# Sparse attention and a token mix on one core: stores and loads of x by 32 rows, two tiles of normalised sums, the mix's first steps in the fixed order, and a weight decode with an addition by GpSimd

## The chip, the cores and the metric

The kernel runs on one core of a Trainium2 chip. A core has five engines that work side by side, each through its own instructions in order: TensorE (PE, with its weight loads shown apart as PEld), VectorE (DVE), ScalarE (ACT), GpSimd (POOL) and SyncE (SP), which here only issues transfers. Sixteen DMA engines move data between the device's memory and SBUF. The metric is the device time of one execution in microseconds. Three timed runs of the kernel before gave 680.64, 686.46 and 686.54 us (median 686.46).

## What is computed

Block-sparse attention over 4 batches, 8 heads, 768 positions and head size 64, followed by a token mix over x, the attention's output with its heads side by side (512 channels). Positions fall into 24 blocks of 32. A query block sees its neighbours, the first and the last block, and three sampled blocks; the first and the last query block see everything.

```python
scores = scale * np.matmul(q, k.transpose(0, 1, 3, 2))
mask = np.abs(blk_i - blk_j) <= window                     # window = 1
mask = mask | (blk_i == 0) | (blk_j == 0) | (blk_i == n_blocks - 1) | (blk_j == n_blocks - 1)
# ... and the three sampled key blocks of each query block
scores = np.where(mask, scores, -1000000000.0)
attn = np.exp(scores - np.max(scores, axis=-1, keepdims=True))
attn = attn / (np.sum(attn, axis=-1, keepdims=True) + 1e-09)
x = np.matmul(attn, v)                                     # heads side by side: (4, 768, 512)

theta = x @ w_theta
zr, zi = x * np.cos(theta), x * np.sin(theta)
y = np.einsum('ts,bsd->btd', w_tok_r, zr) + np.einsum('ts,bsd->btd', w_tok_i, zi)
u = x + y
out = u + np.maximum(u @ w_ch, 0.0)
```

All inputs are float32, but the four weight matrices of the mix reach the core as 64-bit words (two 32-bit words for each value) and are decoded there, each into a high and a low part, whose products (three for each matrix product) give nearly full precision.

## The kernel before

**Attention.** The 4 batches are two pairs `bp`. For each pair there are four *wide* units (the first and last query block, which see all 24 key blocks: one unit for each batch `b` and half of the heads `pp`) and 22 units `i` of one inner query block, all 16 heads of the two batches at once. The list `units` holds these 52 in order, and the loop over `n` runs them in software-pipelined steps under `manual_schedule`: within it the order of the code is the order on each engine. In step `n`:

- `gather_k(n + 2)` copies the key blocks of a unit from the resident `kb` into `kg` (POOL), and `gather_v(n + 2)` fetches the value rows by an indirect DMA that POOL issues (L265);
- `scores(n + 1)` multiplies (S, L282), VectorE reduces to the row bound `m` (L285), and `weights(n + 1)` takes exponentials on ScalarE (P, L294);
- `turn(n)` transposes the weights on PE (T, L300), and ScalarE copies them to `pT` (L302);
- in odd units `values` multiplies the weights of the last two units with their values (X, L333), a *round* of two units; `finish` adds 1e-9 to the row sums, takes the reciprocal and multiplies into the tile `xo` (L319), which exists once (`bufs=1`, L317), and SP stores it to `xs` in the device's memory in two DMAs of 64 rows (L350), each over two query blocks. The store of the wide units (L405) is cut the same way.

SP also issues, in the order of the steps, the loads of q, of the adjoining values (`va`), of the resident keys (`kb`, L222; the second pair's four loads reuse the first pair's space) and of the weights' words.

**The decode of the weights.** `Piece` turns 512 columns (256 for `w_ch`) of 64-bit words into high and low parts. The Decoder spreads three phases a piece over the steps: `ahead` issues `start` (ScalarE, L63) and `high` (ScalarE's cast, L80) before the step's scores, `go` issues `bits`, `rest` and `low` (VectorE, L67 to L84) after its transposes. Seven VectorE operations a piece: three in `bits`, two in `rest` (L75, L77), two in `low` (L83, L84). 22 pieces are decoded in attention and 8 (`w_ch`) in the mix. A piece's words are loaded when the piece two before has ended its third phase.

**The token mix** is a generator, `token_mix`. Its first part allocates what fits while attention's left pools still exist, loads x for two steps (`load_raw` as rows by head for the transposes, L560; `load` as tokens, L547), and does `turn(0)`, `turn(1)`, `theta(0)`, `theta(1)`; after a yield it opens the remaining pools in attention's memory and runs 48 steps (batch, half of the channels, block of 128 tokens): `theta` (L586 to L588), the angles' sine and cosine, `turned` (x times these, split in two parts), and `mix` (L624 to L626) into four accumulators, at each half's end `add_x`; `out` multiplies with `w_ch` (L647 to L649) and stores. This part's order is made by a planner with a cost model. The first part is called (`next(follow)`, L514) after the fixed order has ended, so the planner also places it among attention's last instructions.

`load` reads, for one step, four DMAs by head group `p`: 128 rows of 128 floats; `xs` is laid out as [pair, block, 2, 32 rows, batch, 2, 128].

Of the kernel before, what the change touches and what calls it, by code (L numbers as in the profile page):

```python
# [25 lines left out]
Q_BUFS = 3  # L26
RAW_AHEAD = 6
# [18 lines left out]
class Piece:  # L46
# [14 lines left out]
    def start(self):  # L61
        self.a = self.pool.tile([P, self.f], F32, tag="da", name=f"da_{self.name}", bufs=2)
        self.nc.scalar.activation(self.a, self.raw[:, :, 1].bitcast(F32), AF.Abs, scale=2.0**-16)  # L63

    def bits(self):
        nc, a, ai = self.nc, self.a, self.a.bitcast(I32)
        nc.vector.tensor_scalar(a, a, WORD_LO, WORD_HI, op0=ALU.max, op1=ALU.min)  # L67
        nc.vector.tensor_scalar(ai, ai, 4, 1, op0=ALU.logical_shift_left, op1=ALU.logical_shift_right)
        nc.vector.scalar_tensor_tensor(ai, self.raw[:, :, 1], SIGN_BIT, ai, op0=ALU.bitwise_and, op1=ALU.bitwise_or)

    def rest(self):

        nc = self.nc
        s = self.pool.tile([P, self.f], I32, tag="ds", name=f"ds_{self.name}")
        nc.vector.tensor_scalar(s, self.a.bitcast(I32), EXP_BITS, None, op0=ALU.bitwise_and)  # L75
        low = self.raw[:, :, 0]
        nc.vector.scalar_tensor_tensor(low.bitcast(F32), low.bitcast(U32), 2.0**-52, s.bitcast(F32), op0=ALU.mult, op1=ALU.mult)  # L77
# [4 lines left out]
    def low(self):  # L82
        self.nc.vector.tensor_tensor(self.a, self.a, self.hi.bitcast(F32), op=ALU.subtract)  # L83
# [33 lines left out]
class Tables:  # L117


    def __init__(self, nc, cp, sampled):  # L120
        self.raw = cp.tile([P, NB * 6], I32, name="sb_raw")
        nc.sync.dma_start(self.raw, sampled.rearrange("i k -> (i k)").partition_broadcast(P))

    def make(self, nc, cp):
        raw = self.raw
        words = raw.rearrange("p (i k w) -> p i k w", k=3, w=2)
        given = cp.tile([P, 3, NB], F32, name="sb_given")
        nc.vector.tensor_copy(given, words[:, :, :, 0].rearrange("p i k -> p k i"))
        r = cp.tile([P, 3, NB], F32, name="sb_r")
# [655 lines left out]
```

## Time and profile before

| | before |
|---|---|
| timed runs | 680.64, 686.46, 686.54 us, median 686.46 |
| profiled execution | 681.48 us, its span 679.7 us |
| instructions | 16671 |
| PE busy | 576.1 us (85%) |
| VectorE busy | 448.6 us (66%) |
| ScalarE busy | 334.9 us (49%) |
| POOL busy | 140.6 us (21%) |
| DMA | 95.57 MB, mean 141 GB/s |

The span is what the hardware profiler saw of one execution; 1.8 us lie around it. Busy shares are means over two stages that differ: POOL and most of the DMA traffic belong to attention, and the mix is TensorE's. In the profile a line such as "51.21 0.70 DVE xo L319" gives start, duration, engine, tile and line; what stands in brackets after a timeline entry is the idle time before it and who ended it. "SPq" is the issue of a transfer by SP.

### The profile page before, as it was taken

What the parts mean: (1) busy time and instruction counts of PE and PEld (TensorE: products, weight loads), DVE (VectorE), ACT (ScalarE), POOL (GpSimd) and SP (SyncE); (2) the same over time, 40 slices, a digit from 0 to 9 for tenths busy, and PEclk for the clock granted to TensorE, in tenths of its full rate; (3) what the DMA queues carried; (4) which work ended last, traced back from release to release, by engine and by line L of the source; (5) the groups of instructions that cost most, each with busy time, mean ns of one, the idle gap of its engine ahead of it and who ended that gap; (6) DMA issues with size and microseconds to landing.
All of it is one profiled execution on the core that took longest, in us unless ns stands there. A gap on an engine that the chain in (4) does not pass through costs nothing.

```text
span 679.7 us, 16671 instructions
## 1 busy us (share of the span) xinstructions
PE 576.1 (85%) x6592; PEld 501.7 (74%) x6592; DVE 448.6 (66%) x1063; ACT 334.9 (49%) x708; POOL 140.6 (21%) x262
## 2 busy tenths in 40 slices
PE   4788767585878777774879999999999999999996
PEld 2466445462655545543769999999999999999996
DVE  3797775463777657655389979666586765846654
ACT  3466546362656455544266575345553455533520
POOL 1457546322247454620000000000000000000000
PEclk9989789786989879995769999999999999999999
DMA  8778668665579656742344323421133211121102
GB/s 300 257 224 237 212 208 261 219 213 191 175 231 274 194 180 201 250 140 78 92 123 120 107 56 83 123 78 59 48 95 108 68 58 47 60 69 62 31 0 94
DMA packets 71110, 95.57 MB, mean 141 GB/s; under 512 B 5240, under 2 KB 52984, under 8 KB 71032
## 3 DMA queue, kind: packets, MB, share of 16 engines
q1 hardware_dynamic: 64696, 71.08, 33.3%
q0 software_dynamic: 6336, 23.43, 10.6%
q8 instruction: 52, 0.85, 0.5%
q14 instruction: 26, 0.21, 0.1%
HBM read 81.90 MB, written 12.58 MB: 139 GB/s over the span
## 4 chain that ended last, share of the span: by engine, by line
PE 48%; DMA 34%; DVE 10%; SPq 3%; ACT 3%; issue 2%; DVEq 0%; ACTq 0%
DMA xs<-xo 26%; PE y L624 9%; PE y L625 9%; PE y L626 9%; PE h L588 3%; PE h L586 3%; PE h L587 3%; PE o L647 3%; PE o L648 3%; PE o L649 3%; PE SW L367 3%; DMA kb<-in_kT_dram 2%; DVE xo L319 2%; SPq L350 2%; DMA va<-in_vr_dram 1%
## 5 line engine op out<-in xcount | busy, mean ns | idle before, releaser
L243 POOL COPY kg<-kb 128x256 f32 (+2 forms) x202 | 94.9, 510 | 62.2 <-PE S L282 25.7
L294 ACT ACTIVATE P<-S,m 128x256 f32<-128x256 f32 x176 | 69.1, 477 | 77.4 <-DVE m L285 69.9
L300 PE MATMUL T<-ident,P 128*128 128x128 f32 x352 | 56.3, 312 | 19.9 <-ACT pT L302 19.4
L586 PE MATMUL h<-w_theta_hi,xTh 128*128 128x256 f32 x192 | 56.7, 295 | 14.9 <-ACT P L294 11.7
L624 PE MATMUL y<-w_tok_r_hi,zh 128*128 128x384 f32 x192 | 66.1, 344 | 3.7 <-DVE xo L319 3.3
L300 PEld LDWEIGHTS T<-ident,P 128*128 128x128 f32 x352 | 45.1, 160 | 31.9 <-ACT pT L302 28.9
L333 PE MATMUL X<-vb,pT 128*32 128x65 f32 x1408 | 45.0, 244 | 24.9 <-DVE xo L319 24.8
L625 PE MATMUL y<-w_tok_r_lo,zh 128*128 128x384 f32 x192 | 65.6, 342 | 0.0
L626 PE MATMUL y<-w_tok_r_hi,zl 128*128 128x384 f32 x192 | 64.8, 337 | 0.0
L625 PE MATMUL y<-w_tok_i_lo,zh 128*128 128x384 f32 x192 | 64.7, 337 | 0.0
L624 PE MATMUL y<-w_tok_i_hi,zh 128*128 128x384 f32 x192 | 64.7, 337 | 0.0
L265 POOL DMA_INDIRECT vb<-in_vr_dram,rows x44 | 43.8, 995 | 93.0 <-PE X L333 87.4
L626 PE MATMUL y<-w_tok_i_hi,zl 128*128 128x384 f32 x192 | 62.2, 334 | 0.0
L302 ACT COPY pT<-T 128x1024 f32<-128x1024 f32 x44 | 44.9, 1020 | 33.5 <-PE T L300 33.2
L285 DVE TENSOR_REDUCE m<-S 128x2 f32<-128x512 f32 x88 | 56.2, 680 | 5.9 <-PE S L282 5.9
L333 PEld LDWEIGHTS X<-vb,pT 128*32 128x32 f32 x1408 | 28.5, 119 | 42.0 <-DVE xo L319 32.0
L319 DVE TENSOR_TENSOR xo<-X,sm 128x512 f32<-128x512 f32 x22 | 15.2, 692 | 64.9 <-DMA xs<-xo 62.7
L588 PE MATMUL h<-w_theta_hi,xTl 128*128 128x256 f32 x192 | 56.3, 293 | 1.4 <-DVE xTl L578 1.4
L587 PE MATMUL h<-w_theta_lo,xTh 128*128 128x256 f32 x192 | 56.0, 292 | 0.0
L282 PE MATMUL S<-kg,q 64*32 64x256 f32 x1408 | 53.0, 410 | 3.3 <-DVE q L217 2.0
L586 PEld LDWEIGHTS h<-w_theta_hi,xTh 128*128 128x128 f32 x192 | 38.3, 199 | 16.1 <-ACT P L294 11.9
L333 PE MATMUL X<-va,pT 128*64 128x65 f32 x704 | 44.6, 255 | 0.7 <-DMA va<-in_vr_dram 0.6
(127 smaller groups left out, 1303.6 us busy)
## 6 DMA issues: line engine op xcount, KB each, us to landing
xa<-xs SPq DMA_DIRECT2D x192, 64.0 KB
vw<-in_vr_dram SPq DMA_DIRECT2D x8, 780.0 KB
kb<-in_kT_dram SPq DMA_DIRECT2D x8, 768.0 KB
xr<-xs SPq DMA_DIRECT2D x96, 64.0 KB
out_dram<-of SPq DMA_DIRECT2D x32, 192.0 KB
va<-in_vr_dram SPq DMA_DIRECT2D x22, 260.0 KB
q<-in_qT_dram SPq DMA_DIRECT2D x22, 256.0 KB
xs<-xo SPq DMA_DIRECT2D x44, 128.0 KB
```

Of the source, the lines that this page charges most:

```text
L243: nc.gpsimd.tensor_copy(dst, blocks.rearrange("r g s f -> r s g f"))
L282: nc.tensor.matmul(sc[32 * p : 32 * p + 32, e, b, :], q[rows, b, p, :], keys[rows, :, :, 4 * b + p, :], start=True, stop=True)
L285: nc.vector.tensor_reduce(m[:, e], sc[:, e], axis=AX.X, op=ALU.min)
L294: nc.scalar.activation(pt[:, e, b, :], sc[:, e, b, :], AF.Exp, bias=m[:, e, b : b + 1], scale=-1.0)
L300: nc.tensor.transpose(t[:, k, :], pt, ident)
L333: nc.tensor.matmul(x[r0 : r0 + 32 * n, b, 2 * (p // 2) + e, :], pT_pair[:, 4 * c + 2 * e + b, p, u0 : u0 + n, :], v[:, v0 : v0 + 65], star ...
L586: nc.tensor.matmul(ps, hi[:, c, :], wh[:, c, :], start=c == 0, stop=False)
L587: nc.tensor.matmul(ps, hi[:, c, :], wl[:, c, :], start=False, stop=False)
L588: nc.tensor.matmul(ps, lo[:, c, :], wh[:, c, :], start=False, stop=c == 3)
L624: nc.tensor.matmul(acc, zh[:, dd], wh[:, j, tt], start=j == 0 and m == 0, stop=False)
L625: nc.tensor.matmul(acc, zh[:, dd], wl[:, j, tt], start=False, stop=False)
L626: nc.tensor.matmul(acc, zl[:, dd], wh[:, j, tt], start=False, stop=j == 5 and m == 1)
```

## The change

- `xo` has two buffers. `Tables`, small work at the start, puts its scratch tiles into one of them.
- The stores of `xo` are cut into four DMAs of 32 rows, one for each query block and half of the partitions, where there were two of 64. Heads are regrouped: the half of the partitions is now `p // 2` (before, `p % 2`), and a row of `xs` holds the heads accordingly; keys and values are laid out by the host to match (`place`, `kT`, `va`).
- The mix's `load` is four DMAs of 32 rows with two runs of 256 floats a row, where each had 128 rows of 128 floats.
- The first part of `token_mix` is split by a further yield and moved into the fixed order: pools and the sixteen loads at step `n == len(units) - 2`; `turn`, the load of the sine table, and `theta` of steps 0 and 1 in the last unit's step, before its `finish`.
- The decode: ScalarE makes a second tile from the lower words (`Copy` with a scale, to an integer), `bits` puts the sign into that tile, and `rest` is one integer addition on GpSimd in place of two VectorE operations; `low` is one VectorE operation in place of two. VectorE has four operations a piece. The words of a piece are loaded when the piece two before has done its `bits`.

```diff
+XO_BUFS = 2
@@ Piece
     def start(self):
-        self.nc.scalar.activation(self.a, self.raw[:, :, 1].bitcast(F32), AF.Abs, scale=2.0**-16)
+        self.nc.scalar.activation(self.a, self.raw[:, :, 1].bitcast(F32), AF.Abs, scale=2.0**-48)
+        self.r = self.pool.tile([P, self.f], I32, tag="ds", name=f"ds_{self.name}")
+        self.nc.scalar.activation(self.r, self.raw[:, :, 0].bitcast(U32), AF.Copy, scale=2.0**-29)
     def bits(self):
         nc.vector.tensor_scalar(a, a, WORD_LO, WORD_HI, op0=ALU.max, op1=ALU.min)
-        nc.vector.tensor_scalar(ai, ai, 4, 1, op0=ALU.logical_shift_left, op1=ALU.logical_shift_right)
-        nc.vector.scalar_tensor_tensor(ai, self.raw[:, :, 1], SIGN_BIT, ai, op0=ALU.bitwise_and, op1=ALU.bitwise_or)
+        nc.vector.tensor_scalar(ai, ai, 3, None, op0=ALU.logical_shift_left)
+        nc.vector.scalar_tensor_tensor(r, self.raw[:, :, 1], SIGN_BIT, r, op0=ALU.bitwise_and, op1=ALU.bitwise_or)
     def rest(self):
-        nc.vector.tensor_scalar(s, self.a.bitcast(I32), EXP_BITS, None, op0=ALU.bitwise_and)
-        low = self.raw[:, :, 0]
-        nc.vector.scalar_tensor_tensor(low.bitcast(F32), low.bitcast(U32), 2.0**-52, s.bitcast(F32), op0=ALU.mult, op1=ALU.mult)
+        ai = self.a.bitcast(I32)
+        self.nc.gpsimd.tensor_tensor(ai, ai, self.r, op=ALU.add)
     def low(self):
-        self.nc.vector.tensor_tensor(self.a, self.a, self.hi.bitcast(F32), op=ALU.subtract)
-        self.nc.vector.tensor_tensor(self.lo, self.a, self.raw[:, :, 0].bitcast(F32), op=ALU.add)
+        self.nc.vector.tensor_tensor(self.lo, self.a, self.hi.bitcast(F32), op=ALU.subtract)
@@ Decoder.go
-            if k % 3 == 2 and k // 3 + 2 < len(self.pieces):
+            if k % 3 == 0 and k // 3 + 2 < len(self.pieces):
                 self.pieces[k // 3 + 2].load(self.pool, self.queue)
@@ Tables
-        self.raw = cp.tile([P, NB * 6], I32, name="sb_raw")
+        self.scratch = wp.tile([P, 8, 64], F32, tag="xo", name="sb_scratch", bufs=XO_BUFS).rearrange("p g d -> p (g d)")
+        self.raw = self.part(0, NB * 6).bitcast(I32)
...
@@ attention
-    with ExitStack() as ctx, ExitStack() as early:
+    with ExitStack() as ctx, ExitStack() as scored, ExitStack() as early:
-        ps_s = early.enter_context(tc.tile_pool(name="ps_s", bufs=2, space=PSUM, side="right"))
+        ps_s = scored.enter_context(tc.tile_pool(name="ps_s", bufs=2, space=PSUM, side="right"))
+        def place(b, p):
+            return 4 * b + 2 * (p % 2) + p // 2
-            xo = wp.tile([P, 8, 64], F32, tag="xo", name=f"xo{name}", bufs=1)[:, 0:n]
+            xo = wp.tile([P, 8, 64], F32, tag="xo", name=f"xo{name}", bufs=XO_BUFS)[:, 0:n]
@@ finish
             for c in range(2):
-                nc.sync.dma_start(xs[bp, i : i + 2, c].rearrange("u q b p f -> u q (b p f)"), xo[64 * c : 64 * c + 64])
+                for u in range(2):
+                    r0 = 64 * c + 32 * u
+                    nc.sync.dma_start(xs[bp, i + u, c].rearrange("q b p f -> q (b p f)"), xo[r0 : r0 + 32])
@@ finish_wide
-                    nc.sync.dma_start(xs[bp, 0 : NB : NB - 1, c, :, b].rearrange("z q p f -> z q (p f)"), xo[64 * c : 64 * c + 64])
+                    for z in range(2):
+                        r0 = 64 * c + 32 * z
+                        nc.sync.dma_start(xs[bp, (NB - 1) * z, c, :, b].rearrange("q p f -> q (p f)"), xo[r0 : r0 + 32])
@@ the loop over the steps
             for n in range(len(units) + 1):
+                if n == len(units) - 2:
+                    early.close()
+                    next(follow)
...
                     decoder.go(phases)
+                    if n == len(units) - 1:
+                        scored.close()
+                        next(follow)
                     if last:
                         finish(*last)
...
-        early.close()
-        next(follow)
@@ token_mix
-        ps_h = ctx.enter_context(tc.tile_pool(name="ps_h", bufs=3, space=PSUM, side="right"))
-        ps_o = ctx.enter_context(tc.tile_pool(name="ps_o", bufs=1, space=PSUM, side="right"))
-        tc.keep_in_program_order(nc.scalar.activation(early, half_pi, AF.Sin))
@@ load
-            for p in range(4):
-                src = xs[b // 2, 4 * j : 4 * j + 4, p % 2, :, b % 2, p // 2]
-                nc.sync.dma_start(xa[k][:, p].rearrange("s c u -> s (c u)"), src)
+            for i in range(4):
+                src = xs[b // 2, 4 * j + i, :, :, b % 2].rearrange("c q p f -> q c (p f)")
+                dst = xa[k][32 * i : 32 * i + 32].rearrange("s (c p) x u -> s c (p x u)", c=2)
+                nc.sync.dma_start(dst, src)
@@ the first part
         for k in range(2):
             load_raw(k, xp)
             load(k)
+        yield
+        ps_h = ctx.enter_context(tc.tile_pool(name="ps_h", bufs=3, space=PSUM, side="right"))
+        ps_o = ctx.enter_context(tc.tile_pool(name="ps_o", bufs=1, space=PSUM, side="right"))
         turn(0)
         turn(1)
+        nc.scalar.activation(early, half_pi, AF.Sin)
         theta(0)
         theta(1)
         yield
```

More of the change, by code (lines that the diff above doesn't have):

```diff
@@ L26 @@
 Q_BUFS = 3
+XO_BUFS = 2
 RAW_AHEAD = 6
-WORD_LO = float(np.array([768 << 20], np.uint32).view(np.float32)[0])
-WORD_HI = float(np.array([(1022 << 20) | 0xFFFFF], np.uint32).view(np.float32)[0])
+WORD_LO = float(np.array([512 << 20], np.uint32).view(np.float32)[0])
+WORD_HI = float(np.array([(766 << 20) | 0xFFFFF], np.uint32).view(np.float32)[0])
 SIGN_BIT = -(1 << 31)
-EXP_BITS = -(1 << 23)
 C1 = 6.28125
@@ L117, with __init__, part @@
 class Tables:
-    def __init__(self, nc, cp, sampled):
-        self.raw = cp.tile([P, NB * 6], I32, name="sb_raw")
+    def __init__(self, nc, wp, sampled):
+        self.scratch = wp.tile([P, 8, 64], F32, tag="xo", name="sb_scratch", bufs=XO_BUFS).rearrange("p g d -> p (g d)")
+        self.raw = self.part(0, NB * 6).bitcast(I32)
         nc.sync.dma_start(self.raw, sampled.rearrange("i k -> (i k)").partition_broadcast(P))
+    def part(self, c0, n):
+        return self.scratch[:, c0 : c0 + n]
     def make(self, nc, cp):
@@ L126, in make @@
         words = raw.rearrange("p (i k w) -> p i k w", k=3, w=2)
-        given = cp.tile([P, 3, NB], F32, name="sb_given")
+        given = self.part(144, 72).rearrange("p (k i) -> p k i", k=3)
         nc.vector.tensor_copy(given, words[:, :, :, 0].rearrange("p i k -> p k i"))
-        r = cp.tile([P, 3, NB], F32, name="sb_r")
+        r = self.part(216, 72).rearrange("p (k i) -> p k i", k=3)
         nc.vector.tensor_scalar(r, given, 0.0, float(NB - 1), op0=ALU.max, op1=ALU.min)
@@ L132, in make @@
         nc.vector.tensor_copy(self.block.rearrange("p (i k) -> p k i", k=3), r[0:1])
-        iota_i = cp.tile([P, NB], I32, name="iota_i")
+        iota_i = self.part(288, NB).bitcast(I32)
         nc.gpsimd.iota(iota_i, pattern=[[1, NB]], base=0, channel_multiplier=0)
-        qi = cp.tile([P, NB], F32, name="qi")
+        qi = self.part(312, NB)
         nc.gpsimd.tensor_copy(qi, iota_i)
@@ L141, in make @@
             nc.gpsimd.memset(rows[96:128, :, i], int(ZEROS))
-        first_i = cp.tile([96, NP], I32, name="first_i")
+        first_i = self.part(336, NP)[0:96].bitcast(I32)
         for k in range(3):
             nc.gpsimd.iota(first_i[32 * k : 32 * k + 32], pattern=[[768, NP]], base=0, channel_multiplier=1)
-        first = cp.tile([96, NP], F32, name="first_row")
+        first = self.part(338, NP)[0:96]
         nc.gpsimd.tensor_copy(first, first_i)
@@ L281, in scores @@
                         rows = slice(64 * e, 64 * e + 64)
-                        nc.tensor.matmul(sc[32 * p : 32 * p + 32, e, b, :], q[rows, b, p, :], keys[rows, :, :, 4 * b + p, :], start=True, stop=True)
+                        nc.tensor.matmul(sc[32 * p : 32 * p + 32, e, b, :], q[rows, b, p, :], keys[rows, :, :, place(b, p), :], start=True, stop=True)
             m = wp.tile([P, 2, 2], F32, tag="m", name=f"m{bp}_{i}", bufs=3)
@@ L329, in values, with weigh @@
             va = vas[((i - 1) // 2) % VA_BUFS]
-            def weigh(b, e, p, c, u0, n, v, start, stop):
-                r0 = 64 * (p % 2) + 32 * u0
-                v0 = 65 * (8 * b + 4 * (p // 2) + 2 * e + p % 2)
+            def weigh(b, e, p, k, u0, n, v, start, stop):
+                c, pp = p // 2, p % 2
+                r0 = 64 * c + 32 * u0
+                v0 = 65 * (8 * b + 4 * pp + 2 * e + c)
                 nc.tensor.matmul(
-                    x[r0 : r0 + 32 * n, b, 2 * (p // 2) + e, :], pT_pair[:, 4 * c + 2 * e + b, p, u0 : u0 + n, :], v[:, v0 : v0 + 65],
+                    x[r0 : r0 + 32 * n, b, 2 * pp + e, :], pT_pair[:, 4 * k + 2 * e + b, p, u0 : u0 + n, :], v[:, v0 : v0 + 65],
                     start=start, stop=stop,
@@ L339, in values @@
                 for pp in range(2):
-                    heads = [(b, e, 2 * pp + c) for b in range(2) for c in range(2)]
+                    heads = [(b, e, 2 * c + pp) for b in range(2) for c in range(2)]
                     for head in heads:
@@ L365, in scores_wide @@
                     for e in range(2):
-                        rows, p = slice(64 * e, 64 * e + 64), 2 * pp + c
+                        rows, p = slice(64 * e, 64 * e + 64), 2 * c + pp
                         nc.tensor.matmul(
-                            scs[e][64 * c : 64 * c + 64, 32 * c0 : 32 * (c0 + n)], qe[rows, b, p, :], kb[rows, 4 * b + p, c0 : c0 + n, :],
+                            scs[e][64 * c : 64 * c + 64, 32 * c0 : 32 * (c0 + n)], qe[rows, b, p, :], kb[rows, place(b, p), c0 : c0 + n, :],
                             start=True, stop=True,
```

12 lines of the change are left out of this document (5 added, 7 removed).

## The prediction

> **What bounds the kernel now.** I read the page's chain of waits first, since busy shares are averages over two stages that differ: attention (0 to about 325 us), then the token mix.
>
> ```profile
> PE 48%; DMA 34%; DVE 10%; SPq 3%; ACT 3%; issue 2%; DVEq 0%; ACTq 0%
> DMA xs<-xo 26%; PE y L624 9%; PE y L625 9%; PE y L626 9%; PE h L588 3%; PE h L586 3%; PE h L587 3%; PE o L647 3%; PE o L648 3%; PE o L649 3%; PE SW L367 3%; DMA kb<-in_kT_dram 2%; DVE xo L319 2%; SPq L350 2%; DMA va<-in_vr_dram 1%
> ```
>
> A quarter of the span runs through the stores of `xo`. The table of stretches separates the stages (columns: length, then busy time and count of PE, PEld, DVE, ACT, POOL, granted clock, DMA share, GB/s):
>
> ```profile
> 50.00:299.00 249.00, 187.38 (x3730) 129.71 (x3728) 160.37 (x296) 132.39 (x248) 122.77 (x217) 0.87 0.67 215
> 400.00:500.00 100.00, 100.00 (x630) 100.00 (x629) 70.59 (x190) 50.49 (x119) 0.00 (x0) 1.00 0.26 76
> ```
>
> The mix is TensorE without a gap at full clock: nothing done to its loads or decode can shorten its steady part. In attention no engine is full; PE is busy 75% at clock 0.87. The chain in order of time shows why, and the list of waits who pays:
>
> ```profile
> 51.21 0.70 DVE xo L319
> 51.93 0.51 SPq L350
> 52.50 9.97 DMA xs<-xo
> 62.59 0.70 DVE xo L319
> ```
>
> ```profile
> POOL vb L265 <- PE X L333: 87.4, 19, 10.9
> ACT P L294 <- DVE m L285: 69.9, 34, 8.1
> DVE xo L319 <- DMA xs<-xo: 62.7, 17, 8.8
> ```
>
> With one `xo` tile, L319 waits until the previous store has landed. Behind it in VectorE's order stands the reduction `m`, behind that ScalarE's exponentials, and PE's X waits for the sums tile that L319 frees. A round (two units: 2 S, 2 T, one X) is thus 0.70 + 0.51 + about 10 us.
>
> The timeline gives the length of rounds with and without that wait, from the T that follows each X:
>
> ```profile
> 49.98 1.09 PE L300 MATMUL T<-ident,P 128*128 128x128 f32 x8
> 57.46 1.09 PE L300 MATMUL T<-ident,P 128*128 128x128 f32 x8
> 149.40 1.09 PE L300 MATMUL T<-ident,P 128*128 128x128 f32 x8
> 206.71 1.09 PE L300 MATMUL T<-ident,P 128*128 128x128 f32 x8
> 214.20 1.09 PE L300 MATMUL T<-ident,P 128*128 128x128 f32 x8
> 302.84 1.09 PE L300 MATMUL T<-ident,P 128*128 128x128 f32 x8
> ```
>
> 49.98 to 149.40 are nine rounds of 11.05 us, 206.71 to 302.84 nine of 10.68: mean 10.86. The first round of each half, in which L319 meets no large store in flight, took 7.48 and 7.49 us. That is the round which this PE order reaches when nothing blocks it.
>
> **The stores.** Two edits meet here: two tiles, and 32 rows by store. Two tiles alone only let a store take two rounds. Whether the transfer itself gets shorter is read where little else moves (issues with KB each, then the chain at the end of attention and of the kernel):
>
> ```profile
> xs<-xo SPq DMA_DIRECT2D x44, 128.0 KB
> out_dram<-of SPq DMA_DIRECT2D x32, 192.0 KB
> ```
>
> ```profile
> 318.13 7.96 DMA xs<-xo
> 328.74 7.69 DMA xs<-xo
> 669.07 1.85 DMA out_dram<-of
> ```
>
> A pair's 256 KB took 7.7 to 8.0 us there, against 1.85 us for 192 KB over 128 partitions: near 33 against 104 KB per us. The narrow path is the store's own, not the memory. Old stores begin with a dimension of 2 (`u`, or `z`), new ones with 32 rows. I take the new pair's store at the other row's rate, 256/104 = 2.5 us (bounds 1.85 and 8.0), well inside two rounds. The Trainium skill (DMA: Bandwidth & Descriptors, section on why a DMA increments its semaphore by 16, "How many engines") says that the engine count is the largest number up to 16 dividing the slowest dimension of both sides. By that rule the old stores used 2 engines and the new use 16; the 33 against 104 agrees, though no row counts engines.
>
> **The decode.** Rows by line, for 512-column pieces:
>
> ```profile
> L75 DVE TENSOR_SCALAR ds_tok_r<-da_tok_r 128x512 int32<-128x512 int32 x9 | 4.0, 448 | 0.1
> L77 DVE SCALAR_TENSOR_TENSOR raw_tok_r<-raw_tok_r,ds_tok_r 128x512 f32<-128x512 uint32 x9 | 6.4, 711 | 0.3
> L83 DVE TENSOR_TENSOR da_tok_r<-da_tok_r,w_tok_r_hi 128x512 f32<-128x512 f32 x9 | 7.0, 776 | 0.0
> L63 ACT ACTIVATE da_tok_r<-raw_tok_r 128x512 f32<-128x512 f32 x9 | 6.3, 702 | 0.0
> L243 POOL COPY kg<-kb 128x512 f32<-128x512 f32 x26 | 17.1, 668 | 36.5 <-DMA kb<-in_kT_dram 20.9 <-DMA q<-in_qT_dram 15.5
> ```
>
> VectorE loses three of seven operations: 0.45 + 0.71 + 0.78 = 1.94 us a piece. ScalarE gains one like L63, 0.70 us. POOL gains an integer addition, which the trace doesn't show. Two groups of the same five copies, and a round of POOL without a blocked store:
>
> ```profile
> 230.81 1.98 POOL L243 COPY kg<-kb 128x512 f32<-128x512 f32 x5
> ```
>
> ```profile
> 206.69 0.96 POOL L265 DMA_INDIRECT vb<-in_vr_dram,rows  x1 [2.73 <-PE X L333]
> 207.65 2.04 POOL L243 COPY kg<-kb 128x256 f32<-128x256 f32 x4
> 209.84 0.97 POOL L265 DMA_INDIRECT vb<-in_vr_dram,rows  x1 [0.16 <-issue]
> 210.82 3.13 POOL L243 COPY kg<-kb 128x512 f32<-128x512 f32 x5
> ```
>
> Bounds of the addition: below, 0.67 us (POOL's copy of this size, one input); above, 2 x 0.67 x 3.13/1.98 = 2.1 us, two inputs in the crowded form. I take two inputs, 1.34, nearer to the uncrowded row. By the Trainium skill (GPSIMD Engine Reference, side-by-side accounting: 4497 ns at 2048 elements, VectorE half that) an estimate is 1.1 us, and that page advises VectorE for such work; the sum would move by under 4 us.
>
> 22 pieces make 66 phases over a weight of 56 (44 units, six wide ones counting 2): 66/56 x 2/3 = 0.79 pieces a round. So per round VectorE -1.5 us, ScalarE +0.55, POOL +1.06. POOL's unblocked round above, 206.69 to 213.95, is 7.26 us, with the additions 8.3. New waits: the addition waits for VectorE's `bits`, with the key copies and gathers queued behind it on POOL; ScalarE's cast `high` waits for the addition, with exponentials behind. Mostly these phases lie a unit apart, which covers both. The raw load now waits on `bits` instead of `low`, earlier. SP issues two more stores a round, 2 x 0.51 us, with `va` and `q` loads behind; POOL's and PE's order leave them a round to land.
>
> **Round after:** between PE's 7.5 and POOL's 8.3 I take 8.2. The others fit, scaling the stretch 50:299 by 10.86/8.2 = 1.32: DMA 0.67 to 0.89, VectorE 0.64 to 0.85 less 0.19, ScalarE 0.53 to 0.70 plus 0.07. Gain: 18 x (10.86 - 8.2) = **48 us** (7.5: 60; 9.3: 28).
>
> **The second wide stage** (the chain, then PE in the timeline):
>
> ```profile
> 146.00 0.51 SPq L350
> 147.78 11.53 DMA kb<-in_kT_dram
> ```
>
> ```profile
> 159.44 2.96 PE L367 MATMUL SW<-kb,qe 64*64 64x512 f32 x16 [8.95 <-DMA kb<-in_kT_dram]
> ```
>
> SP issues these keys only after the store at 146.00, which itself waited for L319, and they land beside it. Without the wait they go out a few us earlier relative to PE's work and don't share the store's path: of 8.95 I take **8** (2 to 9). Cheaper decode ahead of the row sums in the two wide stages: at most 1.94 each, **3** (0 to 4).
>
> **The mix's first steps.** In the timeline (PE and VectorE):
>
> ```profile
> 311.18 0.89 DVE L576 STREAM_TRANSPOSE r<-xr 128x128 f32<-128x128 f32 x4 [8.26 <-DMA xr<-xs]
> 315.58 0.58 PE L586 MATMUL h<-w_theta_hi,xTh 128*128 128x256 f32 x1 [11.65 <-ACT P L294]
> 328.28 0.66 PE L624 MATMUL y<-w_tok_r_hi,zh 128*128 128x384 f32 x1 [3.33 <-DVE xo L319]
> ```
>
> The planner put the transposes ahead of the last reduction; they waited for loads not yet landed, and PE stood 11.65 us. The change issues the sixteen loads a round earlier, when key space is free, and turns and multiplies after the last T. From the last T row to the first mix matmul were 25.4 us; without that wait 13.8. Sixteen issues at about 0.5 us now stand on SP ahead of the store of the pair before the last; the second tile covers that. Theta stands ahead of the last X: if the loads are late, X waits too and the gain is gone. I take **11.5** (5 to 13).
>
> ```profile
> 340.00:350.00 10.00, 6.50 (x28) 5.29 (x27) 9.61 (x35) 5.67 (x13) 0.00 (x0) 0.69 0.37 92
> ```
>
> Here 28 matmuls ran where the steady mix runs 63, some 5.5 us lost, because the next loads waited for the store at 328.74 (7.69 us) whose memory they reuse, and VectorE was full. A shorter store and decode give **4** (0 to 7). Wider elements in `xa` loads: nothing, PE covers them.
>
> **Sum:** 48 + 8 + 3 + 11.5 + 4 = 74.5, from the profiled execution's 681.5 (span 679.7): 607. Its runs were 680.6 to 686.5, median 686.5, so the profile sits at the low end; allowing 2 of those 5 us, **609**.
>
> **Rivals.**
> - *The additions land on the path.* POOL is the fullest engine by this sum, and while its copies ran the slow forms appeared (3.13 us above). If each addition also holds up VectorE for its length, the round is 7.26 + 0.79 x 2 x 1.34 = 9.4: 18 x 1.46 + 26.5 = 53 gained, **629**. The Trainium skill (SBUF — State Buffer, port-pair lock) makes VectorE's two-input operations and POOL exclude each other. Against: VectorE has room and drops two such operations. 0.2.
> - *Stores stay narrow.* Then each round still pushes 8 us of store through a path that loads share, the round stays near 10, kb and early mix gain nothing: 18 x 0.86 + 14.5 = 30, **651**. The two rates above speak against. 0.08.
> - *Slower:* a slow integer addition on POOL, in front of gathers and copies. The gains are gone when 18 x (7.26 + 0.79t - 10.86) = 26.5, at t = 6.4 us; at 10 us it ends near **732**. No POOL row here is that long; but none is an integer addition of two tensors. 0.04.
> - *No change:* another wait of 10 us replaces the store's. The 7.48 us rounds speak against. 0.04.
>
> **Numbers.** Forecast 0.64 (594 to 620). The range 594 to 640 adds the first rival. Three runs spread by 0.9%, so 1% is what can be told: faster 0.92, within 1% 0.04, slower 0.04.
>
> **What would show it.** In the profile after: no wait of L319 on `xs<-xo`; T rows 8.2 us apart; a quiet store under 3 us; the addition near 1.3 us; SW's wait for `kb` under 2 us; first mix matmul about 14 us after the last pair's T; the stretch 400:500's density unchanged. Wrong if rounds stay over 9.5, if POOL shows idle time charged to VectorE's `bits` ahead of its gathers, or theta still waits for `xr`.

## The result, and the profile after

The changed kernel takes 620.12 us (median of 4 runs, 617.19 to 624.08), against 686.5 for the kernel before in its 4 runs (680.64 to 690.85): a ratio of 0.906 with a 95% interval of 0.8975 to 0.915. The forecast was 609, its range 594 to 640. The profiled execution took 618.81 us, its span 616.9; before these were 681.48 and 679.7, so 62.8 us of span went.

The chain of waits after, by engine and by line; the stores, which carried 26% before, are no longer among its first lines:

```profile
PE 67%; DVE 11%; DMA 8%; ACT 5%; issue 4%; POOL 2%; POOLq 1%; SPq 1%; DVEq 0%; ACTq 0%
PE y L636 10%; PE y L637 10%; PE y L638 10%; PE X L340 7%; PE T L306 4%; PE S L288 4%; PE h L600 3%; PE h L598 3%; PE h L599 3%; PE o L659 3%; PE o L661 3%; PE o L660 3%; PE SW L376 3%; ACT pT L308 2%; DVE q L219 2%
```

The table of stretches after, with the columns of the one before:

```profile
50.00:299.00 249.00, 210.94 (x4085) 152.91 (x4064) 170.14 (x336) 169.12 (x332) 145.39 (x239) 0.93 0.77 240
400.00:500.00 100.00, 100.00 (x634) 100.00 (x634) 66.56 (x177) 50.18 (x120) 0.00 (x0) 1.00 0.24 71
```

The steady mix runs 634 matmuls in 100 us where it ran 630: unchanged, as forecast. The first row spans the end of attention too, which comes earlier now, so it is not a row of like work. Rows of like work are the two runs of nine rounds and the first 30 us from the first mix matmul, before and then after:

```profile
49.98:149.40 99.42, 76.58 (x1588) 53.75 (x1585) 63.20 (x118) 52.50 (x102) 52.19 (x94) 0.85 0.69 220
206.71:302.84 96.13, 74.00 (x1589) 51.44 (x1585) 63.31 (x118) 52.07 (x102) 53.90 (x94) 0.91 0.65 208
328.28:358.28 30.00, 25.43 (x115) 24.02 (x116) 18.87 (x64) 13.20 (x32) 0.00 (x0) 0.68 0.39 110
```

```profile
48.59:130.51 81.92, 68.98 (x1589) 47.47 (x1585) 56.85 (x103) 57.69 (x115) 61.38 (x102) 0.98 0.92 286
182.40:260.48 78.08, 68.71 (x1588) 47.47 (x1585) 57.68 (x99) 56.69 (x112) 61.44 (x102) 0.98 0.82 255
277.53:307.53 30.00, 30.00 (x186) 30.00 (x187) 25.48 (x82) 21.12 (x55) 4.50 (x6) 0.94 0.59 168
289.25:299.25 10.00, 10.00 (x71) 10.00 (x70) 9.72 (x33) 8.38 (x24) 2.21 (x3) 1.00 0.64 180
```

In the rounds PE stands still for 22 us where it stood for 45, and the same matmuls take 137.7 us of PE where they took 150.6, at a granted clock of 0.98 against 0.85 and 0.91. So about a third of what the rounds gained came with the higher clock. The last row begins 11.7 us after the first mix matmul, as the prediction's 340:350 did before: 71 matmuls run there in place of 28.

The timeline of PE after, at the ends of the stages that the prediction sums:

```profile
48.59 1.09 PE L306 MATMUL T<-ident,P 128*128 128x128 f32 x8
130.51 1.09 PE L306 MATMUL T<-ident,P 128*128 128x128 f32 x8
133.62 1.94 PE L376 MATMUL SW<-kb,qe 64*64 64x512 f32 x5 [2.02 <-DMA kb<-in_kT_dram]
182.40 1.09 PE L306 MATMUL T<-ident,P 128*128 128x128 f32 x8
260.48 1.09 PE L306 MATMUL T<-ident,P 128*128 128x128 f32 x8
262.73 1.09 PE L306 MATMUL T<-ident,P 128*128 128x128 f32 x8 [1.16 <-ACT pT L308]
265.50 0.58 PE L598 MATMUL h<-w_theta_hi,xTh 128*128 128x256 f32 x1 [1.67 <-ACT xTh L589]
277.53 0.41 PE L636 MATMUL y<-w_tok_r_hi,zh 128*128 128x384 f32 x1 [2.97 <-DVE xo L325]
```

Set against the rows of before, the T rows and the first mix matmul cut the span into pieces (us):

| | before | after | gained | forecast |
|---|---|---|---|---|
| start to the first of these T | 49.98 | 48.59 | 1.4 | wide stages together: keys 8, |
| between the halves (second wide stage) | 57.3 | 51.9 | 5.4 | cheaper decode 3, in all 11 |
| twice nine rounds | 195.5 | 160.0 | 35.5 | 48 |
| last pair's T to the first mix matmul | 25.4 | 17.05 | 8.4 | 11.5 |
| first mix matmul to the end | 351.4 | 339.4 | 12.0 | 4 |

A round takes (81.92 + 78.08)/18 = 8.89 us, where 8.2 was forecast and 10.86 was the rule. The transfers of the new stores, in the table of issues (count, KB each, median us to landing) and in the view of the tile `xo`:

```profile
xs<-xo SPq DMA_DIRECT2D x88, 64.0 KB, 4.0
```

```profile
DMA to landing us min/median/max: 1.7/4.0/8.7
```

Now the quickest 64 KB land in 1.7 us, and half of them within 4.0, between the loads of a busier stage. For the last pair, whose store stands in the chain after 328.74 with 7.69 us before, the chain has:

```profile
278.76 2.51 DMA xs<-xo
```

That is the quiet store under 3 us that the prediction asked for; with its four issues, from 277.41 on, the pair takes 3.9 us. L325 waits for no store.

The groups by line and the waits of GpSimd show what is new:

```profile
L76 POOL TENSOR_TENSOR da_tok_i<-da_tok_i,ds_tok_i 128x512 int32<-128x512 int32 x9 | 11.6, 1284 | 19.1 <-DVE ds_tok_i L71 19.1
```

```profile
POOL da_tok_i L76 <- DVE ds_tok_i L71: 19.1, 3, 12.7
POOL da_tok_r L76 <- ACT w_tok_r_hi L79: 15.4, 2, 15.0
POOL vb L271 <- PE X L340: 14.1, 11, 4.4
...
PE S L288 <- POOL kg L249: 3.0, 5, 1.4
```

The addition takes 1.28 us (forecast 1.34). But GpSimd now stands still ahead of its additions for VectorE's and ScalarE's steps, with what follows queued behind, and the idle time that it used to have ahead of its gathers has shrunk from 87.4 us to 14.1. The two longest of these stops lie in the second wide stage, between the runs of rounds:

```profile
141.80 1.26 POOL L76 TENSOR_TENSOR da_tok_r<-da_tok_r,ds_tok_r 128x512 int32<-128x512 int32 x1 [14.96 <-ACT w_tok_r_hi L79]
155.75 1.32 POOL L76 TENSOR_TENSOR da_tok_i<-da_tok_i,ds_tok_i 128x512 int32<-128x512 int32 x1 [12.69 <-DVE ds_tok_i L71]
```

Within the 18 rounds GpSimd waits for the decode's steps for 17.9 us, in 6 stops, and for PE for 14.1 us, where it was 83.9. So most of its slack has gone, though it is busy for only 122.8 of the 160 us. Idle time charged to `bits` was one of the prediction's signs of being wrong.

### The profile page after: what moved, and what is told of

Its sections match the earlier page's. It is cut to its first block, busy times and chain, and to the rows that moved or that the text cites. A ratio compares the mean times of both kernels' runs of the same rounds, so it can differ in the third digit from the quotient of the medians.

```text
span 616.9 us, 16738 instructions
## 1 busy us (share of the span) xinstructions
PE 558.7 (91%) x6592; PEld 487.5 (79%) x6592; DVE 416.5 (68%) x973; ACT 348.0 (56%) x738; POOL 170.8 (28%) x292
## 4 chain that ended last, share of the span: by engine, by line
PE 67%; DVE 11%; DMA 8%; ACT 5%; issue 4%; POOL 2%; POOLq 1%; SPq 1%; DVEq 0%; ACTq 0%
PE y L636 10%; PE y L637 10%; PE y L638 10%; PE X L340 7%; PE T L306 4%; PE S L288 4%; PE h L600 3%; PE h L598 3%; PE h L599 3%; PE o L659 3%; PE o L661 3%; PE o L660 3%; PE SW L376 3%; ACT pT L308 2%; DVE q L219 2%
## 5 line engine op out<-in xcount | busy, mean ns | idle before, releaser
L249 POOL COPY kg<-kb 128x256 f32 (+2 forms) x202 | 87.5, 475 | 15.8 <-DMA q<-in_qT_dram 15.7
L300 ACT ACTIVATE P<-S,m 128x256 f32<-128x256 f32 x176 | 69.2, 487 | 24.9 <-DVE sm L321 14.3
L306 PE MATMUL T<-ident,P 128*128 128x128 f32 x352 | 51.1, 291 | 15.4 <-ACT pT L308 14.4
L306 PEld LDWEIGHTS T<-ident,P 128*128 128x128 f32 x352 | 40.1, 147 | 27.1 <-ACT pT L308 24.1
L598 PE MATMUL h<-w_theta_hi,xTh 128*128 128x256 f32 x192 | 55.1, 287 | 1.7 <-ACT xTh L589 1.7
L602 ACT ACTIVATE t<-h,up_int 128x256 f32<-128x256 f32 x48 | 22.6, 472 | 53.7 <-PE h L600 53.6
L271 POOL DMA_INDIRECT vb<-in_vr_dram,rows x44 | 46.8, 1064 | 19.4 <-PE X L340 14.1
L340 PE MATMUL X<-vb,pT 128*32 128x65 f32 x1408 | 42.8, 229 | 6.7 <-issue 6.5
L340 PEld LDWEIGHTS X<-vb,pT 128*32 128x32 f32 x1408 | 26.6, 110 | 23.2 <-issue 13.4
L609 ACT ACTIVATE cs<-rr 128x256 f32<-128x256 f32 x48 | 20.0, 416 | 42.7 <-DVE rr L607 42.6
L660 PE MATMUL o<-ul,w_ch_hi 128*128 128x384 f32 x128 | 42.8, 334 | 0.0
```

Source lines behind the costliest of these rows:

```text
L249: nc.gpsimd.tensor_copy(dst, blocks.rearrange("r g s f -> r s g f"))
L300: nc.scalar.activation(pt[:, e, b, :], sc[:, e, b, :], AF.Exp, bias=m[:, e, b : b + 1], scale=-1.0)
L306: nc.tensor.transpose(t[:, k, :], pt, ident)
L340: nc.tensor.matmul(x[r0 : r0 + 32 * n, b, 2 * pp + e, :], pT_pair[:, 4 * k + 2 * e + b, p, u0 : u0 + n, :], v[:, v0 : v0 + 65], start=star ...
L598: nc.tensor.matmul(ps, hi[:, c, :], wh[:, c, :], start=c == 0, stop=False)
L660: nc.tensor.matmul(ps, wh[:, c, :], ul, start=False, stop=False)
```

## The experiments

Three questions: was it the narrow path of the stores (theory A), or the second tile and the fixed order of the first steps; why do rounds take 8.89 us rather than 8.2; and where do the 12 us of the mix come from. Every run below was timed beside the kernel before on the same chip. The stages are read from one profiled execution of each, at the same rows as in the table above (round = mean of the same 18 rounds; wide = second wide stage; seam = last pair's T to first mix matmul; mix = the rest).

| run | us | ratio to before (95%) | round | wide | seam | mix |
|---|---|---|---|---|---|---|
| before | 686.5 | 1 | 10.86 | 57.3 | 25.4 | 351.4 |
| changed kernel | 620.1 | 0.906 (0.8975 to 0.915) | 8.89 | 51.9 | 17.0 | 339.4 |
| e1 | 668.5 | 0.975 (0.9705 to 0.9786) | 10.97 | 56.2 | 19.3 | 344.2 |
| e2 | 620.7 | 0.905 (0.9002 to 0.909) | 8.60 | 57.0 | 18.8 | 340.4 |
| e3 | 627.3 | 0.917 (0.9098 to 0.9234) | 8.57 | 52.5 | 18.7 | 352.1 |
| e4 | 629.2 | 0.917 (0.9109 to 0.9228) | 9.05 | 51.2 | 21.1 | 344.5 |
| e5 | 617.8 | 0.896 (0.8925 to 0.8994) | 8.62 | 47.4 | 18.8 | 343.9 |
| e6 | 610.1 | 0.887 (0.8825 to 0.8907) | 8.29 | 49.4 | 18.6 | 341.8 |
| e7 | 625.2 | 0.907 (0.904 to 0.9094) | 8.85 | 51.2 | 18.3 | 344.9 |
| e8 | 609.3 | 0.883 (0.8796 to 0.8864) | 8.30 | 52.5 | 18.4 | 341.1 |
| e9 | 629.3 | 0.914 (0.9101 to 0.9179) | 9.50 | 52.8 | 16.3 | 340.7 |
| e10 | 626.0 | 0.912 (0.9087 to 0.9151) | 8.69 | 52.3 | 16.2 | 344.3 |
| e12 | 624.5 | 0.908 (0.9042 to 0.9111) | 8.31 | 56.0 | 18.0 | 345.9 |

The changed kernel, e2, e4 and e10 have the same stores of 32 rows, the same decode and the same edits to attention's engines, but their rounds read 8.60 to 9.05: a stage of a single profile is known to some 0.2 us a round and a few us elsewhere.

**e1: stores of 64 rows in the changed kernel**, everything else kept, the two tiles too.

```diff
-                for u in range(2):
-                    r0 = 64 * c + 32 * u
-                    nc.sync.dma_start(xs[bp, i + u, c].rearrange("q b p f -> q (b p f)"), xo[r0 : r0 + 32])
+                nc.sync.dma_start(xs[bp, i : i + 2, c].rearrange("u q b p f -> u q (b p f)"), xo[64 * c : 64 * c + 64])
```

> The changed kernel with its stores cut as before (two DMAs of 64 rows), all else kept, two tiles of xo among it. Theory A (the store's own path was narrow, and that path limits the round): a quiet store takes 7.7 to 8 us again against about 2 us in the changed kernel, rounds go from 8.9 us to 10 or more, the second keys come late again; 18 x 1.1 + 6 + 5 gives about 650 us. Theory B (only the wait for a single tile cost time, two tiles cover a slow store): rounds stay at 8.9 us, 620 us.

Rounds are back at 10.97 us. L325 no longer stands for a store, but the waits of this run show where the same time went:

```profile
DVE q L219 <- DMA q<-in_qT_dram: 59.0, 15, 10.9
...
PE X L340 <- DMA va<-in_vr_dram: 24.3, 8, 8.9
```

With a second tile the store may take two rounds, and the loads of q and of the adjoining values, issued behind it, come late in its place. This is the prediction's rival of stores that stay narrow, which put it at 651 us and rounds near 10: a second tile alone would have moved the wait, not removed it; it came to 668.5. The rule of the Trainium skill (DMA: Bandwidth & Descriptors, "How many engines") that the forecast weighed gives 2 engines to this form; the 10.97 against 8.89 us of a round agrees with a narrow path, though no row counts engines.

**e2: one tile in the changed kernel** (`XO_BUFS = 1`).

> The changed kernel with a single tile of xo, stores of 32 rows kept. Theory A (a narrow path): a store under load lands in about 4 us after 2 us of issues, so 0.7 + 2 + 4 = 6.7 us fit in a round of 8.9 and a single tile costs little: 620 to 626 us. Theory B (the single tile was the cost): L325 waits on the store again in most rounds, rounds of 10 us or more, 640 us or more.

620.7 us, as with two, though the waits of this run again show L325 behind stores, for 12.3 us in 5 waits. The second tile is worth nothing that shows.

**e3: the kernel before, with only the stores cut by 32 rows** (in `finish` and `finish_wide`, the diff of e1 the other way round).

> The kernel before with one edit, its stores of xo cut into 32 rows; one tile, old decode, old layout, planner for the mix's first steps. Theory A (a narrow path): the store lands in 4 to 5 us, the round is 0.7 + 2 + 4.5 = 7.2 us at the least by this chain, so the other engines set it near 8.9; 18 x 2 + 6 for the keys + 8 for the early mix is about 50 us less, 636 us. Theory B (the tile): rounds of 10 to 11 us, 670 us or more.

627.3 us: this edit alone takes off 8.3% where the whole change takes off 9.4%. Its one tile still makes L319 wait, but briefly:

```profile
DVE xo L319 <- DMA xs<-xo: 12.7, 8, 5.2
```

Before it was 62.7 us in 17 waits. The seam falls from 25.4 to 18.7 with it, without any change to the order of the first steps; the mix stays at 352.1.

**e4: the first steps left to the planner** in the changed kernel.

```diff
-                if n == len(units) - 2:
-                    early.close()
-                    next(follow)
...
-                    if n == len(units) - 1:
-                        scored.close()
-                        next(follow)
...
             assert not decoder.left(), decoder.left()
+        early.close()
+        scored.close()
+        next(follow)
+        next(follow)
```

> The changed kernel with the mix's first steps left to the planner, as before, after the fixed order. If the early loads gave the gain at the seam, a wait of some 8 to 12 us for xr stands ahead of theta again: 628 to 632 us. If the seam was slow only because of the store on the path, the seam stays at 17 us and the time at 620.

629.2 us. The ratio's interval overlaps the changed kernel's, but against e2 on the same chip (0.905, to 0.909) it lies clear, by some 8 us: that is what the fixed order is worth. PE stands 7.78 us ahead of theta here, against 1.67 in the changed kernel. How the 8 us divide is not shown: the seam reads 4 us more and the mix 5, but e3, also in the old order, has a seam of 18.7, as kernels with the fixed order do.

**e5: the old decode** in the changed kernel: `Piece` and its constants as before (seven VectorE operations, none on GpSimd), and the words of a piece loaded after the third phase.

```diff
-            if k % 3 == 0 and k // 3 + 2 < len(self.pieces):
+            if k % 3 == 2 and k // 3 + 2 < len(self.pieces):
```

> The changed kernel with the old decode (seven VectorE operations a piece, no addition on GpSimd, one ScalarE operation fewer), all else kept. Theory C (relief of VectorE is worth its price): rounds get longer, 9.3 us or more, and the early mix loses up to 5 us: 628 to 635 us. Theory D (the additions stand back to back with the key copies and hold VectorE's scaling of q, L219 up to 3.4 us, which delays the exponentials): those long L219 go, and the round is the same or shorter, 8.2 to 8.9: 612 to 622 us.

617.8 us, ratio 0.896: the new decode gains nothing over the old one, and the intervals (to 0.8994, from 0.8975) leave room for a small loss.

**e6: the addition left out**, so that this kernel's weights are not decoded to their values; **e8: the addition on VectorE**.

```diff
-        self.nc.gpsimd.tensor_tensor(ai, ai, self.r, op=ALU.add)
+        self.nc.vector.tensor_tensor(ai, ai, self.r, op=ALU.add)
```

> The changed kernel with the addition left out (the lower words and the sign never reach the weights, so the output is not the reference's). It prices the 22 + 8 additions by themselves. Theory D (they hold VectorE's scaling of q): the L219 of 3.4 us go, rounds fall to 8.3 or less, 608 to 612 us. Theory C (POOL has room, the additions are hidden): 619 to 621 us.

> The changed kernel with the same addition issued on VectorE, where it is not exact, so the output differs a little. VectorE gets 0.79 x 0.7 us more in a round, POOL 1.0 us less. Theory D: 611 to 618 us, L219 never over 2.5 us. Theory C (VectorE's relief matters): 622 to 628 us.

Both come to the same: 610.1 and 609.3 us, ratios 0.887 and 0.883, rounds 8.29 and 8.30. So the addition on GpSimd costs about 2% of the time before (0.906 less 0.883 or 0.887, 13 to 16 us), and the same addition on VectorE nothing that shows. The expectation took VectorE's sum to be inexact. The row shows it made over halves of 16 bits, in one instruction; whether the sum is exact to the last bit, no row shows. The group by line and the wait of GpSimd in e8:

```profile
L76 DVE CUSTOM_DVE_ANT_0 da_tok_r<-da_tok_r,ds_tok_r 128x1024 uint16<-128x1024 uint16 x9 | 7.4, 823 | 0.1
```

```profile
POOL vb L271 <- PE X L340: 40.4, 19, 4.5
```

0.82 us against 1.28, and GpSimd waits for PE ahead of its gathers 19 times again; its stops for the decode's steps are gone. It is the fastest version seen, 0.883 (0.8796 to 0.8864) against the changed kernel's 0.906 (0.8975 to 0.915). Seven of its 18 rounds take 7.48 or 7.49 us, the length that the prediction read from unblocked rounds (four of 18 in the changed kernel). The first two of them, and the end of the ninth round:

```profile
47.76 1.09 PE L306 MATMUL T<-ident,P 128*128 128x128 f32 x8
55.25 1.09 PE L306 MATMUL T<-ident,P 128*128 128x128 f32 x8
62.73 1.09 PE L306 MATMUL T<-ident,P 128*128 128x128 f32 x8
...
123.70 1.09 PE L306 MATMUL T<-ident,P 128*128 128x128 f32 x8
```

**e7: q not scaled on VectorE.** The timeline of the changed kernel shows a scaling of q that takes 3.43 us, while GpSimd runs copies and an addition back to back:

```profile
87.44 3.43 DVE L219 TENSOR_SCALAR q<-q 128x512 f32<-128x512 f32 x1
```

```profile
86.89 2.47 POOL L249 COPY kg<-kb 128x512 f32<-128x512 f32 x5
89.33 1.26 POOL L76 TENSOR_TENSOR da_tok_r<-da_tok_r,ds_tok_r 128x512 int32<-128x512 int32 x1
```

It ends 0.28 us after GpSimd. By line, before and after:

```profile
L217 DVE TENSOR_SCALAR q<-q 128x512 f32<-128x512 f32 x22 | 11.1, 503 | 7.1 <-DMA q<-in_qT_dram 7.1
```

```profile
L219 DVE TENSOR_SCALAR q<-q 128x512 f32<-128x512 f32 x22 | 22.4, 1019 | 3.0 <-DMA q<-in_qT_dram 3.0
```

Is this hold-up (theory D) the cost of the addition? e7 takes the instruction away: the scale goes into the bounds and the exponentials.

```diff
-                nc.vector.tensor_scalar(t, t, -0.125, None, op0=ALU.mult)
...
-                nc.vector.tensor_reduce(m[:, e], sc[:, e], axis=AX.X, op=ALU.min)
+                nc.vector.tensor_reduce(m[:, e], sc[:, e], axis=AX.X, op=ALU.max)
+            nc.vector.tensor_scalar(m, m, -0.125, None, op0=ALU.mult)
...
-                    nc.scalar.activation(pt[:, e, b, :], sc[:, e, b, :], AF.Exp, bias=m[:, e, b : b + 1], scale=-1.0)
+                    nc.scalar.activation(pt[:, e, b, :], sc[:, e, b, :], AF.Exp, bias=m[:, e, b : b + 1], scale=0.125)
```

> The changed kernel without the scaling of q on VectorE: the row bound is the maximum, a small operation on m multiplies it by -0.125, and the exponential has the scale 0.125; the same results. Theory D: the operation that GpSimd holds up is gone, so the waits of PE's T for pT of 2 to 2.5 us (five of them, 11 us) go too, minus 0.3 us a round for the small operation: 608 to 614 us. Without theory D (some other operation is held in its place, such as the decode's two-input ones): 617 to 624 us.

Rounds of 8.85 us and a ratio of 0.907: nothing gained. But this does not settle theory D. The chain of the changed kernel runs through L219 (2% in the page above), through the long one too:

```profile
87.52 3.36 DVE q L219
```

And in e7 the hold-up has only moved, to the small operation on `m`, which ScalarE's exponentials wait for. Its durations (least, median, most, in ns), that wait, and its longest case:

```profile
L290 DVE TENSOR_SCALAR m<-m x44: 169/234/1871, 37.3 to 263.0; 128x4 f32<-128x4 f32 x44
```

```profile
ACT P L299 <- DVE m L290: 11.0, 8, 4.4
```

```profile
220.46 2.47 POOL L247 COPY kg<-kb 128x512 f32<-128x512 f32 x5
222.31 1.87 DVE L290 TENSOR_SCALAR m<-m 128x4 f32<-128x4 f32 x1
222.90 1.26 POOL L76 TENSOR_TENSOR da_tok_i<-da_tok_i,ds_tok_i 128x512 int32<-128x512 int32 x1
```

It ends 0.02 us after the addition. PE's waits of T for pT did fall, from 14.4 us to 6.9, while its waits for the key copies rose from 3.0 to 6.2. So e7 shows only that taking the scaling of q off VectorE gains nothing.

**e9: two additions on GpSimd for each piece.**

```diff
         self.nc.gpsimd.tensor_tensor(ai, ai, self.r, op=ALU.add)
+        self.nc.gpsimd.tensor_tensor(self.r, self.r, ai, op=ALU.add)
```

> The changed kernel, with GpSimd adding twice for each piece of 512 columns: the second addition of the same size writes a tile that nobody reads again, so the output is unchanged and only GpSimd's length grows. 22 more additions of 1.28 us, 0.79 a round (a round is two units of attention), 1.0 us a round. Theory P (GpSimd's order sets the round: each addition and its wait push the gathers and key copies behind it): the 18 rounds grow from the 8.89 us of the changed kernel to 9.6 to 10, the time from 620 to 632 to 640. Rival M (the transfers set the round, share 0.93 of the DMA engines in the rounds): 620 to 626, rounds under 9.2. Rival W (what costs is the wait of the addition on VectorE and ScalarE, not its length): the same 620 to 626.

629.3 us, between the two forecasts; 0.914 against 0.906 with overlapping intervals, so 5 us by the ratios and 9 by the medians. The rounds read 9.50, nearer to theory P, but the profiled execution (634.7 us) was the longest of its four. What does move as theory P says is what PE waits for, its scores behind the key copies:

```profile
PE S L289 <- POOL kg L250: 14.3, 12, 2.8
```

3.0 us in 5 waits with one addition, 14.3 in 12 with two (50 to 276 us); in e8, with none on GpSimd, that wait is not in the list. So GpSimd's order does come to stand ahead of PE, and each addition pushes it further. How much of the first addition's 13 to 16 us is its length, how much the standing still ahead of it and how much the hold-up of VectorE stays open: the second addition, which has no new wait, cost less.

**e10: `xa` loaded as before**, four loads by head in place of four by block.

```diff
-            for i in range(4):
-                src = xs[b // 2, 4 * j + i, :, :, b % 2].rearrange("c q p f -> q c (p f)")
-                dst = xa[k][32 * i : 32 * i + 32].rearrange("s (c p) x u -> s c (p x u)", c=2)
-                nc.sync.dma_start(dst, src)
+            for p in range(4):
+                src = xs[b // 2, 4 * j : 4 * j + 4, p // 2, :, b % 2, p % 2]
+                nc.sync.dma_start(xa[k][:, p].rearrange("s c u -> s (c u)"), src)
```

> The changed kernel, with the mix's tiles xa loaded as before (four loads by head, each with 4 runs of 128 bytes a row, in place of four loads by block with 2 runs of 512 bytes a row). The changed kernel's stretch from the first mix matmul to the end is 339.4 us against 351.4 before; 32-row stores alone leave it at 352.1, the planner's order of the first steps at 344.5, the old decode at 343.9. Theory A (the new cut of these loads carries part of those 12 us): that stretch grows to 343 to 347 and the time to 624 to 628. Rival B (PE covers these loads, as the prediction said): the stretch stays within 1.5 us of 339.4 and the time within 618 to 623.

626.0 us and 344.3 us from the first mix matmul: both numbers lie where theory A put them. It is not shown by them: the ratio's interval overlaps the changed kernel's, and e1, e7 and e12, which keep the new loads, read 344.2 to 345.9. (The expectation has the sizes wrong: a run of the old load is 128 floats, 512 bytes, and of the new one 256 floats, 1 KB.)

**e11 and e12: what holds e8 at 8.30 us**, when PE's own round is 7.48? In e8 the DMA engines are nearly always busy in the first nine rounds (in the other nine their share is 0.91):

```profile
50.00:124.00 74.00, 66.96 (x1547) 46.97 (x1548) 60.99 (x105) 55.37 (x110) 50.79 (x90) 0.98 0.99 297
```

e11 adds 256 KB a round to e8 (with one tile, to make room); e12 takes some 72 KB a round away by decoding more in the wide units.

```diff
+            t = wp.tile([P, 512], F32, tag="more", name=f"more{bp}_{i}", bufs=1)
+            nc.sync.dma_start(t, vr[768 * bp : 768 * bp + 128, 0:512])
```

> The version with the addition on VectorE (609.3 us, rounds of 8.30 us, share of the DMA engines 0.99 in the rounds), with one more load of 256 KB a round into a tile that nobody reads, and one tile of normalised sums to make room for it (worth nothing either way in the changed kernel). Theory M (in the rounds the transfers have become what sets the pace): 256 KB at 297 GB/s are 0.86 us, times 20 to 22 rounds, so the time goes to 623 to 630 and the rounds to 9.0 to 9.3. Rival E (an engine sets the pace: PE's 7.5 us or GpSimd's 7.3): the time stays within 607 to 614, rounds under 8.5.

```diff
-            weight = 0.0 if n < 2 else 2.0 if units[n][1] == "w" else 1.0
+            weight = 0.0 if n < 2 else 4.0 if units[n][1] == "w" else 1.0
```

> The version with the addition on VectorE, with the six wide units counted 4 in place of 2 when the decode is spread: 66 phases over 68 in place of 56, so 0.65 pieces a round in place of 0.79, and the rest into the wide stages, where the DMA engines are busy 0.67 and VectorE 0.66. A try at a faster version. Theory M (transfers set the round): 0.14 pieces of 512 KB less, 72 KB at 297 GB/s, 0.24 us a round, 4 to 5 us in all gained, less what the wide stages lose (0 to 4): 604 to 609. Rival E (an engine sets the pace): VectorE's 0.14 x 5 operations do not show, rounds stay 8.3, and the wide stages lose: 609 to 614.

e11 took 618.2 us (0.896, 0.8894 to 0.9025), between the two forecasts, and its runs spread from 611 to 622. Its interval lies clear above e8's: 256 KB more a round cost some 9 us by the ratios, where theory M asked for 14 at the least, so neither theory is borne out. e12 took 624.5, 15 us more than e8 where either theory allowed 5. Its rounds stay at 8.31, so 72 KB less does not shorten them; the loss lies elsewhere: the first of the T rows comes at 55.5 us instead of 47.8, the second wide stage takes 56.0 instead of 52.5, and the mix 345.9 instead of 341.1. Decoding more in the wide stages pays for itself nowhere. A share of 0.99 of the DMA engines is thus not shown to be the bound. The mean of 8.30 us is made of unblocked rounds and of longer ones in which PE waits, for `pT`, for a cause that the profile doesn't name, and once for `va`:

```profile
PE T L306 <- ACT pT L308: 8.3, 9, 1.3
...
PE X L340 <- issue: 4.9, 4, 1.4
PE X L340 <- DMA va<-in_vr_dram: 2.4, 1, 2.4
```

In the changed kernel the first two were 14.4 us in 8 waits and 6.5 in 5. What stands behind them stays open.

## Why the prediction was right, and where its sizes were off

- **The narrow store (right).** The forecast's main mechanism, a store form that moves a pair's 256 KB in about 8 us and a cut by 32 rows that ends this, is shown by e1 and e3 from both sides. That the second tile hardly matters (e2) is in line with its remark that two tiles alone only give the store more time.
- **Rounds: 48 us forecast, 35.5 got.** The step that failed is the choice of 8.2 us "between PE's 7.5 and POOL's 8.3". Without the addition (e6, e8) the round is 8.3, so 8.2 is the right size for the stores and the freed VectorE, with nothing for GpSimd in it. The addition was entered as 1.06 us more for an engine with room. GpSimd's work came out smaller than its sum, 6.8 us a round (122.8/18) where 7.26 + 1.06 was entered; what the sum had at nothing is GpSimd's standing still for the decode's earlier steps, which the forecast held to be covered, the phases lying a unit apart (17.9 us in the 18 rounds), and for PE. (8.89 - 8.30) x 18 = 10.6 us is what the profiles show, most of the 12.5 missing, as far as single profiles tell: the five kernels with one addition on GpSimd and the new stores read 8.60 to 9.05. So the first rival came true by half: it set rounds of 9.4 us. Its mechanism, an addition that holds up VectorE, is seen in rows of the changed kernel and of e7; what share of the cost it has is open, since e6 and e8 take away this hold-up and GpSimd's stops together.
- **The decode: 3 us forecast in the wide stages, besides VectorE's relief.** e5 shows nothing gained in all. Where it helps (e8 against e5, same chip: 0.883 (0.8796 to 0.8864) against 0.896 (0.8925 to 0.8994), some 9 us) the addition runs on VectorE. The Trainium skill (GPSIMD Engine Reference, section on when to use GPSIMD) sends elementwise additions to VectorE, GpSimd being about half as fast with two inputs; here 1.28 against 0.82 us. The forecast weighed the page's price, under 4 us of its sum, and not the advice, on which 13 to 16 hung.
- **Second wide stage: 11 us forecast with the start, 6.8 got.** Of the keys' wait of 8.95 us, 2.02 is left at that place, about as forecast. The stage reads 47.4 to 57.0 us over the runs, and its remainder isn't settled.
- **Seam: 11.5 forecast, 8.4 got.** The mechanism was half wrong: the forecast put the whole wait down to the planner's order, but e3 takes 6.7 us off in the old order, with PE's wait ahead of theta at 6.13 us in place of 11.65. The fixed order takes that wait to 1.67, yet the seam reads 16.2 to 19.3 in the kernels that have it, so what it adds there is not told from the scatter. Theta still waits 1.67 us for its input, and a T ahead of it 1.16; these two, 2.8 us, are the most of the 3.1 missing.
- **Early mix: 4 forecast, 12 got.** The forecast counted the loss in one stretch of 10 us, 340:350, and took part of it; but the mix was slow over its first 30 us, 115 matmuls where 186 run now, which at the steady 63 in 10 us are 11 us. Of the 30 us PE stood still for 4.6 (25.43 busy); the rest of the loss went with a granted clock of 0.68 against 0.94, some 6 us by an estimate from these rows (busy time times clock: 17.3 against 28.2). The step "a shorter store and decode give 4" also named one wrong cause: e3's shorter stores leave the stretch at 352.1. All edits but the cut of the stores (e1) read 344.2. Putting back the order (e4), the decode (e5) or the `xa` loads (e10) alone makes 344.5, 343.9 or 344.3 of 339.4; but kernels with all three edits read 340.4 to 341.8 (e2, e6, e8, e9) and also 344.2 (e1), 344.9 (e7) and 345.9 (e12). So no share of a single edit is shown, and "wider elements in `xa` loads: nothing" is neither borne out nor refuted. A full VectorE does not tell the two kernels apart: in the matching stretch it is busy 9.72 of 10 us now, 9.61 before.

The times of the rivals (629, 651, 732) leave out the 2 us that the forecast allowed above the profile; the first would be 631.

The total came out 11 us from the forecast because errors of opposite sign met: too much for the rounds (12.5), the wide stage (4) and the seam (3), too little for the mix (8). That they met is luck.

## What to carry to other kernels

Look at the rate of a transfer where nothing else moves, form by form: 256 KB in 8 us beside 192 KB in 1.85 us pointed at the shape of the store, and the one edit that mends the shape (e3) gave most of the gain. A second buffer did not mend it; it handed the wait to the loads behind (e1). Before believing that an experiment took a cause away, see whether its replacement meets the same wait (e7). Before giving work to an engine with idle time, list what that engine waits for and who waits behind it: its slack may be what keeps its in-order queue ahead of the others. And cost an offload against the same operation left where its neighbours run, which here was the better version.

## What the runs showed of the hardware that was not expected

- An addition of int32 on VectorE was made as one instruction over 16-bit halves (128x1024 uint16) in 0.82 us, less than GpSimd's 1.28 us.
- A VectorE instruction of 0.5 us took 3.43 us while GpSimd ran five copies and an addition without a pause, and ended with them. With it removed, the operation in its place, 0.17 us at the least, took 1.87 us in the same way, and no time was gained.
- At a DMA share of 0.99 in nine rounds, 72 KB less a round left the rounds at 8.31 us, while 256 KB more cost some 9 us of the whole.
- Less waiting came with a higher granted clock: 0.85 and 0.91 in the two runs of rounds before and 0.98 after, 0.68 and 0.94 in the first 30 us of the mix, and the matmuls themselves took less time.
